# Windowed attention packed into 64 key columns from unit 3 on, and a buffer of its own for the last plain accumulators

## The chip, the cores and the metric

The program runs on one core of a Trainium2 chip. The metric is device time in microseconds (us); the kernel before takes 845.69 us (median of 3 runs, 845.41 to 848.99). TensorE (PE) multiplies matrices into PSUM, VectorE (DVE) and ScalarE (ACT) do the elementwise work, GpSimd (POOL) makes masks, and SyncE (SP) issues nearly all DMAs from one queue, in order.

## The reference

Three layers follow one another. The first is attention in which every query sees the 64 latest positions of its own sequence, itself included; the other two are feed-forward layers of 2304 tokens.

```python
batch, n_heads, seq, head_dim = (4, 8, 576, 64)
window = 64
scale = 1.0 / np.sqrt(D)
scores = scale * np.matmul(q, k.transpose(0, 1, 3, 2))
rel = pos[:, None] - pos[None, :]
mask = (rel >= 0) & (rel < window)
scores = np.where(mask, scores, -1000000000.0)
scores = scores - np.max(scores, axis=-1, keepdims=True)
attn = np.exp(scores)
attn = attn / (np.sum(attn, axis=-1, keepdims=True) + 1e-09)
x = np.matmul(attn, v)            # as 2304 tokens x 512
h = np.maximum(x @ w_in, 0.0);  x = h * h @ w_out          # d_ff 2048
h = x @ w2_in;                  out = h * np.cos(h) @ w2_out
```

## The kernel before

**The work.** The 2304 tokens are cut into nine units of 256 (n = 0 to 8). Attention runs per unit and per group of four heads (g = 0, 1): 18 calls of `attention`. Tokens of units 0 to 4 then go through the first feed-forward layer in the plain way (`UnitA`: matmuls `ph` into PSUM, a squared ReLU on ACT and DVE, matmuls `accA` into four PSUM accumulators; a block is 12 matmuls of 256 or 512 columns). Units 5 to 8 go through it in a form with fewer products (`group1` and `job1`: tiles x, y, z and `accC`), and the second layer follows in that form too (`group`, `Job`: x, y, z and `accB`). Large matmuls run as three products of high and low parts.

**One attention call.** `scores` makes S: a block of 64 queries against the 128 keys that hold its windows, 16 matmuls on quarters of the array (64 rows by 64 columns), each of which the trace records as two (32 records). `neg_max` adds a mask of 128 columns and takes the maximum (eight DVE instructions of 128x128), `exp` runs eight times over 128 columns on ACT, `recip` and `norm` follow in halves. `transp` turns each half (four transposes of 128x128 each, tile T, two groups a call), `p_copy` takes T to SBUF, and `weighted` multiplies by the values: 16 matmuls, 128 rows of keys by 64 columns, over 64 queries (tile O, 32 records). Two copies, `hi` and `lo`, put O into X; units 7 and 8 go whole into `x_whole` instead.

**The order.** The author writes operations (`op`) with engine costs and a key. A planner (`Plan.run`) sorts them into one fixed order per engine when the program is built; on the chip each engine takes its list in order and waits on semaphores. The keys of the middle stretch (attention of units 3 to 8, the sums `sums1`, the conversions `convert_w2`) stand in the table `MID`. Four PSUM banks (ring "q") are shared by S, T, O, `ph` and x, y, z; four more (ring "acc") hold accumulators, and the first `accC` takes over the banks of the last `accA`.

**The end of the plain layer.** `UnitA.finish` copies each of the four `accA` to SBUF and stores it to DRAM (`x_dram`). The copies go into ring "x2", which has two buffers: the third copy needs the first store to have landed, and the fourth the second. Ring "W" has 18 larger buffers for weights.

Of the kernel before, what the change touches and what calls it, by code (L numbers as in the profile page):

```python
# [9 lines left out]
F32 = mybir.dt.float32  # L10
# [76 lines left out]
class Plan:  # L87
# [12 lines left out]
    def op(self, engs, key, fn, deps=(), take=(), use=(), lat=None, gap=0, order=()):  # L100
        if lat is None:
            lat = self.PE_LAT if "PE" in engs else self.LAT
        o = Op(engs, key, fn, [d for d in (*deps, *order) if d is not None], list(take), lat)
        o.order = [d for d in order if d is not None]
        o.seq, o.gap = len(self.ops), gap
        self.ops.append(o)
        for b in (*take, *use):
            b.users.append(o)
        for b in take:
            b.taker = o  # L110
        o.deps += [b.taker for b in use if b.taker is not None and b.taker not in o.deps]
        return o
# [70 lines left out]
def act_us(n, sbuf=True):  # L183
    return 0.05 + 0.093 * sbuf + n / 1200.0


def dve_us(n, fast=False):
    return 0.065 + n / (1920.0 if fast else 960.0)
# [6 lines left out]
def pe_us(n, passes=1):  # L195
# [3 lines left out]


PER1 = 22.7
MID = {'att': {3: (-1.6, 1.8),
         4: (40.0, 3.7),
         5: (26.6, 6.7),
         6: (27.0, 7.3),
         7: (48.6, 4.5),
         8: (44.7, 0)},
 'sum': (13, 16, 18, 20, 24, 34, 35, 37),
 'w2': (24, 27, 29, 40, 41, 43, 45, 46, 46, 46, 46, 46, 47, 47, 48, 49),
 'w2key': 26.3}  # L210

START = {'ahead': 4,
 'att': {(0, 0): (9.7, 7.0),
# [31 lines left out]
def kernel(  # L245
# [89 lines left out]
    def bank(buf, shape, name):  # L335
        return ps_q.tile([P, *shape], F32, tag=f"q{buf.slot}", name=name)
# [264 lines left out]
    def setup_row_mask(kind):  # L601
        m = ap_.tile([P, P], F32, tag="row_mask_" + kind, bufs=1, name="row_mask_" + kind)
        nc.gpsimd.memset(m, 0.0)
        for rows in HALF:
            nc.gpsimd.affine_select(
                out=m[rows], in_=m[rows], compare_op=ALU.is_ge, fill=-BIG, base=-1,
                pattern=[[1, P]], channel_multiplier=-1,
            )
            nc.gpsimd.affine_select(
                out=m[rows], in_=m[rows], compare_op=ALU.is_ge, fill=-BIG, base=WINDOW,  # L610
                pattern=[[-1, P]], channel_multiplier=1,
            )
        if kind != "n":
            nc.gpsimd.memset(m[HALF["sb".index(kind)], 0:WINDOW], -BIG)
        masks[kind] = m

    def setup_rest(e):
        make_identity(nc, ident)
        nc.gpsimd.memset(hpi, HALF_PI)
        nc.gpsimd.memset(quarter, 0.25)  # L620
# [3 lines left out]
        o_mask[kind] = op({"POOL": 1.3}, -100, lambda e, kind=kind: setup_row_mask(kind))  # L624
    o_setup = op({"POOL": 0.8}, -100, setup_rest)
    o_mask["b"] = op({"POOL": 1.3}, -100, lambda e: setup_row_mask("b"))

    def mask_kind(t):
        if (t * P) % seq == 0:
# [16 lines left out]

    loaded = [None, None]

    def attention(n, g, key, sp, k_s=None):

        nm = f"{n}_{g}"
        t = {}
        turn = {(0, 0): "acc", (0, 1): "guest"}.get((n, g), "q")
# [151 lines left out]
        turns[turn] = o_v  # L805

        cs = slice(2 * g, 2 * g + 2)
        if n >= len(x_col):
            at = (n - len(x_col)) * UA
            new = xr.slot is None and not xr.users  # L810

            def whole(eng):
                if xr.tile is None:
                    xr.tile = wp.tile([P, NCC, H1], F32, tag=f"W{xr.slot}", name="x_whole")
                copy(eng, xr.tile[:, cs, at:at + UA], t["O"])

            o_h = op({"ACT": act_us(2 * UA, False), "DVE": dve_us(2 * UA) + 0.11}, key + sp, whole,
                     [o_v, s1_held[0]], [xr] if new else [], [ob] if new else [ob, xr])
            for r in range(2):
                x_hi[n, 2 * g + r] = x_lo[n, 2 * g + r] = o_h  # L820
            return

        half, off = divmod(x_col[n], 2 * UA)
        sl = slice(off, off + UA)

# [20 lines left out]
    class UnitA:  # L846
# [71 lines left out]
            return (b, []) if j == 0 and m % self.per == 0 else ([], b)  # L918

        def finish(self, key, ends):  # L920
            for i, b_acc in enumerate(self.acc_b):
                b = R["x2"].buf()
                t = {}
                c0 = i * self.per

                def cp_(e, i=i, t=t):
                    t["x"] = ma.tile([P, self.per, self.w], F32, tag="x2", name=f"x2_{self.n}_{i}")
                    if e == "ACT":
                        nc.scalar.activation(t["x"], self.acc[i], AF.Copy)
                    else:  # L930
                        nc.vector.tensor_copy(t["x"], self.acc[i])

                def st(e, c0=c0, t=t):
                    nc.sync.dma_start(
                        x2d[:, c0:c0 + self.per, self.n * UA:self.n * UA + self.w], t["x"])

                o = op({"ACT": act_us(512, False), "DVE": dve_us(512)}, key, cp_,
                       [ends[c0 + self.per - 1]], [b], [b_acc])
                o = dma(key, st, P * 512 * 4, [o], use=[b])
                for n in self.parts:  # L940
                    for c in range(c0, c0 + self.per):
                        x2_done[n, c] = o
# [928 lines left out]
```

## Time and profile before

| | |
|---|---|
| median of 3 runs | 845.69 us |
| the profiled execution, its own time | 845.52 us |
| its span, first to last instruction | 843.4 us |
| PE busy | 833.8 us (99%) |
| DVE busy | 656.1 us (78%) |
| ACT busy | 485.6 us (58%) |
| granted TensorE clock, mean | 0.998 |
| DMA, bytes over the span | 181.91 MB |

The span is 2.1 us shorter than the time of that execution. Busy shares are means over stages. Of the span, 0 to 100 us is the beginning (units 0 to 2, conversion of the first layer's weights), 100 to 292 us the middle (plain layer beside the attention of units 3 to 8), 292 to 475 us the first layer's second form, and from 460 us on the second layer.

### The profile page before, as it was taken

How to read it: one execution, taken by the hardware profiler on the slowest of the kernel's cores; microseconds unless marked ns; L12 is line 12 of the kernel's file. 1: busy time of each engine (PE TensorE's matmuls, PEld its weight loads, DVE VectorE, ACT ScalarE, POOL GpSimd, SP SyncE). 2: the span in 40 equal slices, each digit the busy share in tenths (PEclk: the TensorE clock that was granted, in tenths of full speed). 3: DMA queues.
4: the chain of work that ended last, by engine and by line, in shares of the span. 5: the costliest groups of instructions: out<-in, count | busy, mean ns of one | idle time of the engine just before them, and what ended most of it. 6: DMA issues, size and time to landing. Idle time of an engine off the chain costs nothing.

```text
span 843.4 us, 14086 instructions
## 1 busy us (share of the span) xinstructions
PE 833.8 (99%) x5236; PEld 730.8 (87%) x5236; DVE 656.1 (78%) x1485; ACT 485.6 (58%) x1041; POOL 11.8 (1%) x31
## 2 busy tenths in 40 slices
PE   8999999999999999999999999999999999999998
PEld 8898889998888877888888999988999988999986
DVE  6999987689777975777679788886788885788851
ACT  7998665576767744434422655653565563556542
POOL 2100010000000000000000000000000000000000
PEclk9999999999999999999999999999999999999999
DMA  9884367577775588998899495044643053643010
GB/s 343 325 328 137 141 226 270 223 235 242 289 308 187 185 296 294 349 325 304 307 356 393 172 422 192 1 169 168 227 161 126 1 205 132 249 152 112 1 38 37
DMA packets 39795, 181.91 MB, mean 216 GB/s; under 512 B 4016, under 2 KB 6576, under 8 KB 27440
## 3 DMA queue, kind: packets, MB, share of 16 engines
q1 hardware_dynamic: 39728, 181.03, 58.2%
q8 instruction: 41, 0.67, 0.3%
q14 instruction: 26, 0.21, 0.1%
HBM read 129.63 MB, written 51.38 MB: 215 GB/s over the span
## 4 chain that ended last, share of the span: by engine, by line
PE 95%; ACT 2%; DMA 2%; DVE 0%; issue 0%; SPq 0%; ACTq 0%
PE accB L1246 23%; PE ph L1577 13%; PE x L1288 12%; PE accA L909 12%; PE accC L1494 10%; PE z L1288 6%; PE x L1416 5%; PE y L1288 3%; PE z L1416 2%; PE O L776 2%; PE S L719 2%; PE T L761 2%; PE y L1416 1%; PE accA L970 1%; DMA x_dram<-x 1%; DMA qk<-in_qk_dram 1%
## 5 line engine op out<-in xcount | busy, mean ns | idle before, releaser
L1577 PE MATMUL ph<-X,W_in_w_dram 128*128 128x512 f32 (+1 forms) x624 | 125.0, 345 | 0.0
L909 PE MATMUL accA<-g,W_in_w_dram 128*128 128x512 f32 (+1 forms) x528 | 111.4, 355 | 0.0
L1577 PEld LDWEIGHTS ph<-X,W_in_w_dram 128*128 128x128 f32 x624 | 98.1, 189 | 13.8 <-issue 1.4
L1246 PE MATMUL accB<-wo,gb_e 128*128 128x512 f32 x432 | 100.1, 389 | 0.0
L909 PEld LDWEIGHTS accA<-g,W_in_w_dram 128*128 128x128 f32 x528 | 86.5, 189 | 13.7 <-issue 1.2
L1246 PEld LDWEIGHTS accB<-wo,gb_e 128*128 128x128 f32 x432 | 81.0, 188 | 16.6
L742 ACT ACTIVATE pb<-pb,mm 128x128 f32<-128x128 f32 x144 | 55.8, 389 | 13.3 <-DVE mm L736 13.3
L1246 PE MATMUL accB<-wo,gb_a 128*128 128x512 f32 x216 | 54.2, 393 | 0.0
L1246 PE MATMUL accB<-wo,gb_b 128*128 128x512 f32 x216 | 54.2, 393 | 0.0
L1246 PEld LDWEIGHTS accB<-wo,gb_b 128*128 128x128 f32 x216 | 40.2, 188 | 7.4
L373 ACT ACTIVATE raw_in_w_dram<-raw_in_w_dram 128x1024 f32<-128x1024 f32 x32 | 36.5, 1144 | 17.6 <-DMA raw_in_w_dram<-in_w_dram 17.6
L1246 PEld LDWEIGHTS accB<-wo,gb_a 128*128 128x128 f32 x216 | 40.2, 188 | 7.2
L1304 ACT ACTIVATE held<-x 128x384 f32<-128x384 f32 x72 | 34.3, 481 | 19.9 <-PE x L1288 19.8
L1288 PE MATMUL x<-X,wb 128*128 128x384 f32 x216 | 45.7, 337 | 0.0
L1288 PE MATMUL x<-X,wa 128*128 128x384 f32 x216 | 45.3, 335 | 0.0
L1494 PE MATMUL accC<-g_k,W_in_w_dram 128*128 128x512 f32 x192 | 44.3, 389 | 0.0
L1494 PEld LDWEIGHTS accC<-g_k,W_in_w_dram 128*128 128x128 f32 x192 | 36.0, 188 | 7.3
L1220 DVE TENSOR_TENSOR gb_e<-keep,gb_e 128x384 fp32r<-128x384 f32 x48 | 25.9, 554 | 20.2 <-ACT gb_e L327 20.0
L1288 PEld LDWEIGHTS x<-X,wa 128*128 128x128 f32 x216 | 38.7, 188 | 2.4
L1288 PEld LDWEIGHTS x<-X,wb 128*128 128x128 f32 x216 | 38.5, 188 | 0.3
L1435 ACT ACTIVATE held<-x 128x512 f32<-128x512 f32 x24 | 14.3, 598 | 42.2 <-PE x L1416 42.2
L873 ACT ACTIVATE r<-ph 128x512 f32<-128x512 f32 (+1 forms) x52 | 25.6, 493 | 21.1 <-PE ph L1577 20.5
(194 smaller groups left out, 1713.9 us busy)
## 6 DMA issues: line engine op xcount, KB each, us to landing
raw_in_w_dram<-in_w_dram SPq DMA_DIRECT2D x32, 1024.0 KB, 7.9
wa<-w2a_dram SPq DMA_DIRECT2D x24, 1024.0 KB, 7.7
wb<-w2b_dram SPq DMA_DIRECT2D x24, 768.0 KB, 6.6
qk<-in_qk_dram SPq DMA_DIRECT2D x17, 576.0 KB, 6.4
v<-in_v_dram SPq DMA_DIRECT2D x18, 512.0 KB, 5.9
w1s_dram<-s SPq DMA_DIRECT2D x8, 1024.0 KB, 4.7
w2a_dram<-w2a SPq DMA_DIRECT2D x8, 1024.0 KB, 6.0
w1a<-w1s_dram SPq DMA_DIRECT2D x8, 1024.0 KB, 7.7
```

The costliest lines, as they stand in the source:

```text
L373: nc.scalar.activation(hw, hw, AF.Prelu, scale=2.0**-112, alpha=-(2.0**32))
L719: nc.tensor.matmul(S[e][HALF[c], r, i], t["qk"][HALF[e], r, q0:q0 + WINDOW], t["qk"][HALF[e], r, UA + q0:UA + q0 + P], start=(r == 0 and i ...
L742: nc.scalar.activation(t["pb"][:, e, r, i], t["pb"][:, e, r, i], AF.Exp, bias=t["mm"][:, e, r, i:i + 1], scale=-1.0, accum_out=t["sm"][:, ...
L873: nc.scalar.activation(t["r"], ph()[:, 0:w], AF.Relu)
L909: nc.tensor.matmul(self.acc[i][:, k, :], w[:, j % 2, wl, m * P:m * P + P], t["g"][:, gl, :], start=(j == 0 and p == 0 and k == 0 and self. ...
L1220: nc.vector.tensor_tensor(t["g"][:, 1], r(), f32(t["g"][:, 0]), ALU.subtract)
L1246: nc.tensor.matmul(acc[0], t["g"][:, gl, m * P:m * P + P], wb.tile[:, k % 2, wl], start=(k == 0 and i == 0), stop=(k == NJ - 1 and i == 2))
L1288: nc.tensor.matmul(ps[x], wb.tile[:, i, wl, c * P:c * P + P], piece(o, c, xl), start=(first and c == 0 and k == 0), stop=(last and c == 1 ...
L1304: return b, op({"ACT": act_us(H)}, key - 6, lambda e: nc.scalar.activation(r_at(b), ps[x], AF.Copy), [dep, o_rooms], [b], [buf], lat=0.39)
L1416: nc.tensor.matmul(ps[x], wb.tile[:, i, wl, c * P:c * P + P] if src is pb or i > 1 else wb.tile[:, wl, i, c * P:c * P + P], piece1(o, c, x ...
L1494: nc.tensor.matmul(acc[0][:, 0], wb.tile[:, k % 2, wl, m * P:m * P + P], t["g"][:, gl, :], start=(k == 0 and p == 0), stop=(k == NJ - 1 an ...
L1577: nc.tensor.matmul(t["ph"][:, 0:u.w], wb.tile[:, j % 2, wl, c * P:c * P + P], u.x(xl, c), start=(c == 0 and k == 0), stop=(c == NCC - 1 an ...
```

## The change

Units 0 to 2 keep the old attention. From unit 3 on, twelve calls go to a new function `packed`. A query at place j of its block sees exactly one of the two keys j of the block before and of its own block, for every j; so the 128 columns hold 64 that count. `gather` copies, under a mask, the own-block columns over the others (and a large negative number where a sequence begins, which is in units 4 and 6), and takes the maximum over 64 columns. `exp` reads S in PSUM directly, 64 columns at a time. One group of four transposes turns everything, two products with 0/1 masks (`spread`) set the probabilities apart again, and `weighted` multiplies by the own block and the block before in turn: 32 matmuls of 64 rows by 64 columns, into two banks. Two banks mean two `hi` and two `lo` copies of half the width. In `finish`, the last unit's four copies go into one buffer of ring "W". `MID` has new keys throughout.

```diff
--- before.py
+++ after.py
@@ -199,15 +199,18 @@
 
 
 PER1 = 22.7
-MID = {'att': {3: (-1.6, 1.8),
-         4: (40.0, 3.7),
-         5: (26.6, 6.7),
-         6: (27.0, 7.3),
-         7: (48.6, 4.5),
-         8: (44.7, 0)},
- 'sum': (13, 16, 18, 20, 24, 34, 35, 37),
- 'w2': (24, 27, 29, 40, 41, 43, 45, 46, 46, 46, 46, 46, 47, 47, 48, 49),
- 'w2key': 26.3}
+PACKED = 3
+MASK = I32
+MARGIN = 0.7
+MID = {'att': {3: (-3.1, 3.1),
+         4: (38.0, 3.0),
+         5: (32.8, 5.1),
+         6: (13.5, 7.7),
+         7: (22.0, 2.0),
+         8: (19.0, 3.6)},
+ 'sum': (17, 19, 20, 25, 28, 39, 41, 42),
+ 'w2': (19, 20, 21, 40, 41, 42, 45, 48, 49, 50, 53, 55, 56, 57, 57, 58),
+ 'w2key': 65.5}
...
+    def staircase(name, dtype, cols, turned):
+        m = ap_.tile([P, cols], dtype, tag=name, bufs=1, name=name)
+        nc.gpsimd.memset(m, 1.0)
+        for rows in HALF:
+            for c in range(0, cols, WINDOW):
+                nc.gpsimd.affine_select(
+                    out=m[rows, c:c + WINDOW], in_=m[rows, c:c + WINDOW], compare_op=ALU.is_ge,
+                    fill=0.0, base=0, pattern=[[1 if turned else -1, WINDOW]],
+                    channel_multiplier=-1 if turned else 1)
+        return m
+
+    def opposite(name, dtype, m):
+        o = ap_.tile(list(m.shape), dtype, tag=name, bufs=1, name=name)
+        nc.gpsimd.tensor_scalar(o, m, -1.0, 1.0, ALU.mult, ALU.add)
+        return o
...
+    def packed(n, g, key, sp, k_s=None):
+
+        nm = f"{n}_{g}"
+        t = {}
...
+        sb = [R["q"].buf() for _ in range(2)]
+        tb = R["q"].buf()
+        ob = [R["q"].buf() for _ in range(2)]
...
+        def gather(eng, e):
+            if e == 0:
+                t["mm"] = ap_.tile([P, 2, 2, HB], F32, tag="mm", bufs=2, name=f"mm_{nm}")
+                t["sm"] = ap_.tile([P, 2, 2, HB], F32, tag="sm", bufs=2, name=f"sm_{nm}")
+            S = t["S"][e]
+            nc.vector.copy_predicated(
+                S[:, :, :, 0:WINDOW],
+                masks["own"].unsqueeze(1).unsqueeze(1).to_broadcast([P, 2, HB, WINDOW]),
+                S[:, :, :, WINDOW:P])
+            for i in range(HB):
+                kind = mask_kind(HB * n + i)
+                if kind != "n":
+                    rows = HALF["sb".index(kind)]
+                    nc.vector.copy_predicated(
+                        S[rows, :, i, 0:WINDOW],
+                        masks["prev"][rows].unsqueeze(1).to_broadcast([WINDOW, 2, WINDOW]),
+                        masks["none"][rows].unsqueeze(1).to_broadcast([WINDOW, 2, WINDOW]))
+            nc.vector.tensor_reduce(
+                t["mm"][:, e], S[:, :, :, 0:WINDOW], mybir.AxisListType.X, ALU.max, negate=True)
...
+        def exp(eng, e, r, i):
+            nc.scalar.activation(
+                t["pb"][:, e, r, i], t["S"][e][:, r, i, 0:WINDOW], AF.Exp,
+                bias=t["mm"][:, e, r, i:i + 1], scale=SCALE,
+                accum_out=t["sm"][:, e, r, i:i + 1])
...
+        def norm(eng):
+            pb = t["pb"].rearrange("p e r i q -> p (e r i) q")
+            nc.vector.tensor_tensor(
+                pb, pb, t["sm"].rearrange("p e r i -> p (e r i)").unsqueeze(2)
+                .to_broadcast([P, 4 * HB, WINDOW]), ALU.mult)
+
+        def transp(eng):
+            t["T"] = bank(tb, [2, 2, P], f"T_{nm}")
+            for e in range(2):
+                for r in range(2):
+                    nc.tensor.transpose(
+                        t["T"][:, e, r], t["pb"][:, e, r].rearrange("p i q -> p (i q)"), ident)
+
+        def spread(eng, k):
+            if k == 0:
+                t["pt"] = room("PT", ptb, 2 * DM, [2, 4, P])
+            nc.vector.tensor_tensor(
+                t["pt"][:, k], t["T"].rearrange("p e r q -> p (e r) q"),
+                masks["LU"[k]].unsqueeze(1).to_broadcast([P, 4, P]), ALU.mult)
+
+        def weighted(eng):
+            t["O"] = [bank(b, [2, P], f"O_{nm}_{i}") for i, b in enumerate(ob)]
+            for r in range(2):
+                for c in range(2):
+                    cols = slice(c * WINDOW, c * WINDOW + WINDOW)
+                    for k in range(2):
+                        for i in range(HB):
+                            for e in range(2):
+                                nc.tensor.matmul(
+                                    t["O"][i][HALF[e], r, cols],
+                                    t["v"][HALF[i], c + 1 - k + i, 2 * r + e],
+                                    t["pt"][HALF[i], k, 2 * e + r, cols],
+                                    start=(r == c == k == 0), stop=(r == c == k == 1),
+                                    skip_group_check=True)
+
...
+        late = key + sp
+        o_r = op({"DVE": 0.42}, late, recip, ex, use=[smb])
+        o_n = op({"DVE": dve_us(512) + 0.02}, late, norm, [o_r], use=[smb, pbuf], lat=MARGIN)
+        o_t = op({"PE": 4 * pe_us(P) + 0.09}, late, transp, [o_n, o_setup], [tb], [pbuf])
+        o_p = []
+        for k in range(2):
+            first = k == 0
+            o_p.append(op({"DVE": dve_us(512)}, late, lambda q, k=k: spread(q, k), [o_t, o_pack[2], *o_p],
+                          [ptb] if first else [], [tb] if first else [tb, ptb], lat=MARGIN))
+        free = ([s1_held[0]] if n >= len(x_col) else [g1_last[m] for m in x_before[n]]) if g else []
+        o_v = op({"PE": 0.35 + 16 * 0.053}, late, weighted, [l1, *o_p, *free], [*ob], [ptb, vb])
+        turns["q"] = o_v
...
     def attention(n, g, key, sp, k_s=None):
-
+        if n >= PACKED:
+            return packed(n, g, key, sp, k_s)
...
         def finish(self, key, ends):
+            apart = self.n == spans[-1][0]
+            whole = R["W"].buf() if apart else None
             for i, b_acc in enumerate(self.acc_b):
-                b = R["x2"].buf()
+                b = whole or R["x2"].buf()
                 t = {}
                 c0 = i * self.per
 
                 def cp_(e, i=i, t=t):
-                    t["x"] = ma.tile([P, self.per, self.w], F32, tag="x2", name=f"x2_{self.n}_{i}")
+                    if apart:
+                        t["x"] = part1(whole, "x2_apart", i).rearrange("p (k n) -> p k n", k=1)
+                    else:
+                        t["x"] = ma.tile([P, self.per, self.w], F32, tag="x2", name=f"x2_{self.n}_{i}")
                     if e == "ACT":
                         nc.scalar.activation(t["x"], self.acc[i], AF.Copy)
                     else:
@@ -935,7 +1142,8 @@
                         x2d[:, c0:c0 + self.per, self.n * UA:self.n * UA + self.w], t["x"])
 
...
                 o = op({"ACT": act_us(512, False), "DVE": dve_us(512)}, key, cp_,
-                       [ends[c0 + self.per - 1]], [b], [b_acc])
+                       [ends[c0 + self.per - 1]], [] if apart and i else [b],
+                       [b_acc, b] if apart and i else [b_acc])
                 o = dma(key, st, P * 512 * 4, [o], use=[b])
```

On PE, at the second call of unit 7 (names: T_7_1 is a transpose group of unit 7, group 1; O_7_1 its weighted sum; S_8_0 the next call's scores), the program before has two transpose groups, and the scores directly behind the weighted sum:

```order
L761 MATMUL T_7_1_0_3148<-ident_77,pb_7_1_3066 128x128 x4
L1577 MATMUL ph_45_3136<-X_80,W_in_w1_dram_8_962 128x512 x6
L909 MATMUL accA_3_0_2562<-g_43_3042,W_in_w1_dram_7_897 128x512 x3
...
L761 MATMUL T_7_1_1_3191<-ident_77,pb_7_1_3066 128x128 x4
L1577 MATMUL ph_46_3197<-X_80,W_in_w1_dram_10_967 128x512 x6
L776 MATMUL O_7_1_3205<-PT_7_1_3158,v_7_1_3099 64x64 x16
L719 MATMUL S_8_0_0_3223<-qk_8_0_3112 64x128 x2
```

The same place of the changed program, where the two rows of O stand eight times in all:

```order
L777 MATMUL T_7_1_3315<-ident_77,pb_7_1_3225 128x128 x4
L1111 MATMUL accA_3_3_2645<-g_44_3166,W_in_w1_dram_9_1024 128x512 x3
L1785 MATMUL ph_47_3330<-X_80,W_in_w1_dram_10_967 128x512 x9
L795 MATMUL O_7_1_0_3345<-PT_7_1_3326,v_7_1_3216 64x64 x2
L795 MATMUL O_7_1_1_3346<-PT_7_1_3326,v_7_1_3216 64x64 x2
...
L1785 MATMUL ph_47_3330<-X_80,W_in_w1_dram_10_967 128x512 x3
L1111 MATMUL accA_3_0_2623<-g_45_3268,W_in_w1_dram_9_1024 128x512 x3
L723 MATMUL S_8_0_0_3392<-qk_8_0_3253 64x128 x2
```

One transpose group is gone, O has twice the matmuls, and S no longer follows O here; each of the twelve calls' S stood directly behind the O of the call before; now five do, and seven are parted from it like this. The order and number of the large matmuls is otherwise the same, and from the first x of the second form on PE has the same list as before.

On DVE, the same call of the changed program from its scores to its transposed probabilities (g_45 and g_46 belong to the plain layer, w2a and cw to the conversion of the second layer's weights):

```order
L736 COPY_PREDICATED S_7_1_0_3226<-is_own_1436,S_7_1_0_3226 128x4x64
L748 TENSOR_REDUCE mm_7_1_3249<-S_7_1_0_3226 128x4
...
L755 TENSOR_SCALAR mm_7_1_3249<-mm_7_1_3249 128x8
L334 CAST g_45_3268<-r_45_3221 128x512
L1088 TENSOR_TENSOR g_45_3268<-r_45_3221,g_45_3268 128x512
L392 ISA cw_in_w2_dram_4_3223<-raw_in_w2_dram_4_3138,cw_in_w2_dram_4_3223 128x2048
...
L764 TENSOR_SCALAR sm_7_1_3250<-sm_7_1_3250 128x8
L765 RECIPROCAL sm_7_1_3250<-sm_7_1_3250 128x8
L769 TENSOR_TENSOR pb_7_1_3225<-pb_7_1_3225,sm_7_1_3250 128x512
...
L783 TENSOR_TENSOR PT_7_1_3326<-T_7_1_3315,by_own_1450 128x512
L783 TENSOR_TENSOR PT_7_1_3326<-T_7_1_3315,by_prev_1456 128x512
```

In place of eight masked maxima, two reciprocals and two norms stand two selections, two maxima, one reciprocal, one norm and the two products behind T.

At the end of the plain layer ACT made all four copies before (x2_3_0 to x2_3_3 are the copies of accA_3_0 to accA_3_3):

```order
L929 ACTIVATE x2_3_0_3748<-accA_3_0_2562 128x512
L327 ACTIVATE raw_in_w2_dram_7_3692<-raw_in_w2_dram_7_3692 128x1024
L929 ACTIVATE x2_3_1_3766<-accA_3_1_2569 128x512
L327 ACTIVATE g_bg0_3776<-r_bg0_3741 128x512
L929 ACTIVATE x2_3_2_3790<-accA_3_2_2584 128x512
L1435 ACTIVATE held1_3643<-x1_1_3707 128x512
L929 ACTIVATE x2_3_3_3813<-accA_3_3_2595 128x512
```

In the changed program ACT makes three of them, and the second (accA_3_1) stands on DVE, behind a weight conversion (cw) and an addition (hk1):

```order
L1602 TENSOR_TENSOR g1_ag0_3847<-r1_ag0_3840,g1_ag0_3847 128x512
L388 TENSOR_SCALAR cw_in_w2_dram_7_3861<-raw_in_w2_dram_7_3645 128x1024
L392 ISA cw_in_w2_dram_7_3861<-raw_in_w2_dram_7_3645,cw_in_w2_dram_7_3861 128x2048
L1650 TENSOR_TENSOR hk1_3777<-z1_0_3790,held1_3759 128x512
L1138 COPY x2_apart_3863<-accA_3_1_2629 128x512
```

Here g1_ag0 is the operand of the first `accC` matmuls; what moved is the copy that frees the bank of the second `accC`, from ACT to DVE.

## Rows read from the trace of the kernel before

**Rows 1.** The page, part 1: busy us (share of span) xinstructions.

```profile
PE 833.8 (99%) x5236; PEld 730.8 (87%) x5236; DVE 656.1 (78%) x1485; ACT 485.6 (58%) x1041; POOL 11.8 (1%) x31
```

**Rows 2.** Waits of PE: us in total, times, longest.

```profile
PE accC L1494 <- ACT x L929: 2.6, 1, 2.6
```

**Rows 3.** Windows, middle: busy us (xinstructions) of PE, PEld, DVE, ACT, POOL, clock, DMA.

```profile
200.00:250.00 50.00, 50.00 (x452) 40.74 (x451) 41.18 (x130) 33.63 (x98) 0.00 (x0) 1.00 0.73 276
```

**Rows 4.** Timeline of PE over one attention call: start us, us, instruction.

```profile
196.98 1.53 PE L909 MATMUL accA<-g,W_in_w_dram 128*128 128x512 f32 x6
198.35 0.60 PE L761 MATMUL T<-ident,pb 128*128 128x128 f32 x4
198.70 1.64 PE L909 MATMUL accA<-g,W_in_w_dram 128*128 128x512 f32 x6
200.18 1.55 PE L1577 MATMUL ph<-X,W_in_w_dram 128*128 128x512 f32 x6
...
201.92 1.64 PE L1577 MATMUL ph<-X,W_in_w_dram 128*128 128x512 f32 x6
203.50 1.15 PE L776 MATMUL O<-PT,v 128*64 128x64 f32 x32
204.58 1.10 PE L719 MATMUL S<-qk 64*64 64x128 f32 x32
205.61 3.03 PE L909 MATMUL accA<-g,W_in_w_dram 128*128 128x512 f32 x12
208.48 2.89 PE L1577 MATMUL ph<-X,W_in_w_dram 128*128 128x512 f32 x12
```

**Rows 5.** Windows of 20 ns inside that S: PE's (x) counts matmuls in flight.

```profile
204.82:204.84 0.02, 0.02 (x8) 0.02 (x4) 0.02 (x1) 0.02 (x2) 0.00 (x0) 1.00 0.00 0
...
204.86:204.88 0.02, 0.02 (x12) 0.02 (x8) 0.02 (x1) 0.02 (x2) 0.00 (x0) 1.00 0.00 0
...
204.92:204.94 0.02, 0.02 (x8) 0.02 (x4) 0.02 (x1) 0.02 (x1) 0.00 (x0) 1.00 0.00 0
204.96:204.98 0.02, 0.02 (x12) 0.02 (x8) 0.02 (x1) 0.02 (x1) 0.00 (x0) 1.00 0.00 0
```

**Rows 6.** Timeline of PE behind the last O, which no S follows.

```profile
278.73 3.02 PE L909 MATMUL accA<-g,W_in_w_dram 128*128 128x512 f32 x12
281.59 2.88 PE L1577 MATMUL ph<-X,W_in_w_dram 128*128 128x512 f32 x12
```

**Rows 7.** Timeline of PE at the first accC; in brackets idle time and its releaser.

```profile
314.23 0.84 PE L1494 MATMUL accC<-g_ag,W_in_w_dram 128*128 128x512 f32 x3
317.65 0.96 PE L1494 MATMUL accC<-g_ag,W_in_w_dram 128*128 128x512 f32 x3 [2.58 <-ACT x L929]
318.45 2.17 PE L1416 MATMUL x<-X,w1b 128*128 128x512 f32 x6
320.41 2.54 PE L1416 MATMUL x<-X,w1a 128*128 128x512 f32 x6
...
324.17 1.52 PE L1416 MATMUL x<-X,w1b 128*128 128x512 f32 x6
```

**Rows 8.** Windows behind that wait; the clock is the seventh column, after POOL.

```profile
320.00:322.00 2.00, 2.00 (x6) 1.61 (x5) 0.69 (x1) 0.60 (x1) 0.00 (x0) 0.50 1.01 418
```

**Rows 9.** The chain that ended last, ahead of the wait: start us, us, what.

```profile
309.61 7.30 DMA x_dram<-x
```

**Rows 10.** Groups of DVE and ACT by form: busy us, mean ns, idle before.

```profile
L736 DVE CUSTOM_DVE_ANT_0 pb<-S,row_mask_n 128x128 f32<-128x128 f32 x112 | 26.9, 285 | 4.3 <-PE S L719 4.3
L331 DVE COPY PT<-T 128x512 f32<-128x512 f32 x9 | 6.2, 690 | 4.3 <-PE T L761 4.3
L742 ACT ACTIVATE pb<-pb,mm 128x128 f32<-128x128 f32 x144 | 55.8, 389 | 13.3 <-DVE mm L736 13.3
```

**Rows 11.** Timeline of DVE, two like instructions in a row, and a conversion.

```profile
284.41 1.29 DVE L1087 TENSOR_TENSOR piece<-x_tmp,piece 128x512 fp32r<-128x512 f32 x2
309.64 1.22 DVE L389 CUSTOM_DVE_ANT_0 cw_in_w_dram<-raw_in_w_dram,cw_in_w_dram 128x2048 uint16<-128x2048 uint16 x1
```

More of the change, by code (lines that the diff above doesn't have):

```diff
@@ L615, in setup_row_mask, with setup_early, setup_first, setup_late @@
         masks[kind] = m
+    def staircase(name, dtype, cols, turned):
[12 more added lines that the diff above has]
+        return o
+    def setup_early(e):
+        masks["own"] = staircase("is_own", MASK, WINDOW, False)
+    def setup_first(e):
+        masks["prev"] = opposite("is_prev", MASK, masks["own"])
+        masks["none"] = ap_.tile([P, WINDOW], F32, tag="none", bufs=1, name="none")
+        nc.gpsimd.memset(masks["none"], -BIG / SCALE)
+    def setup_late(e):
+        masks["L"] = staircase("by_own", F32, P, True)
+        masks["U"] = opposite("by_prev", F32, masks["L"])
     def setup_rest(e):
@@ L626 @@
     o_mask["b"] = op({"POOL": 1.3}, -100, lambda e: setup_row_mask("b"))
+    o_pack = {}
     def mask_kind(t):
@@ L807, in attention @@
         cs = slice(2 * g, 2 * g + 2)
[L808 to L821, printed above, removed]
         half, off = divmod(x_col[n], 2 * UA)
@@ L926, in cp_ @@
                 def cp_(e, i=i, t=t):
-                    t["x"] = ma.tile([P, self.per, self.w], F32, tag="x2", name=f"x2_{self.n}_{i}")
+                    if apart:
+                        t["x"] = part1(whole, "x2_apart", i).rearrange("p (k n) -> p k n", k=1)
+                    else:
+                        t["x"] = ma.tile([P, self.per, self.w], F32, tag="x2", name=f"x2_{self.n}_{i}")
                     if e == "ACT":
```

80 lines of the change are left out of this document (added).

## The prediction

> **What bounds the kernel now.** I read the page first: PE is busy for 833.8 of 843.4 us [rows 1]. A busy PE need not be a fast one, so I went to PE's own waits and to its timeline. In the waits only one stop of any size stands behind the beginning: 2.6 us ahead of an `accC` [rows 2]. In the timeline the starts tell the rate: six matmuls of 512 columns take 1.37 us from start to start (196.98 to 198.35), 0.228 us each, and they go on like this from block to block [rows 4]. The middle therefore lasts as long as its PE list. The windows of the middle show DVE at 41.18 and ACT at 33.63 of 50 us [rows 3]: crowded, but ahead of PE. So the change is worth three things: what it takes from PE's list, what it does to the one stop, and what new stops it makes. What it saves on ACT or DVE gives nothing by itself.
>
> **The transposes.** From 198.35 to 200.18 PE does one transpose group and six large matmuls [rows 4]; less 1.37 us for the six, the group costs 0.46 us with what it delays behind it. Twelve calls have one group less each: 12 x 0.46 = **5.5 us gained**. No wait hides this, since PE is the engine that all wait for.
>
> **The weighted sum.** O has 32 records now, 64 columns each, and takes 1.08 us (203.50 to 204.58); S has 32 records of 128 columns on four quarters of the array and takes 1.03 us (204.58 to 205.61) [rows 4]. Per tile that is 16 records of 64 columns in 1.08 us for O on its two halves, 68 ns each, and 8 records of 128 columns in 1.03 us for S on its four quarters, 129 ns each. Both are what the columns suggest if every tile works by itself. Slices of 20 ns inside S say so directly: the number of matmuls in flight goes from 8 at 204.82 to 12 at 204.86, is back at 8 at 204.92 and again 12 at 204.96 [rows 5]. Four begin within some 50 ns, then none until the next round. The new O has 64 records of 64 columns, 16 for each of four tiles, so it should again take 16 x 68 ns = 1.08 us: **no cost**. The other bound is that a record costs PE a place of its own, whichever tile it is on; the mean of S is 1.03 / 32 = 32 ns, and 64 x 32 ns = 2.06 us, 0.98 us more per call and 11.8 us for twelve. I take the first end, as the slices show starts far denser than 32 ns.
>
> A page speaks for the other end. The Trainium skill ("TensorE: Matmul & The Clock Gate", section "Wait — 56ns, not 53.3ns?") says that matmuls never start closer than about 25 ns, however few columns they have. By that page O would take an estimated 64 x 25 ns = 1.6 us, and my sum would end at 844.2 us instead of 838.0. The slices of S do not agree with it for matmuls on different tiles; no run here yet shows 64 of them in a row.
>
> **Parted pairs.** Going into O costs 0.10 us (201.92 to 203.50 is 1.58, while the like stretch behind a transpose group, 198.70 to 200.18, is 1.48); the first twelve large matmuls behind S take 2.87 instead of 2.74, so leaving costs 0.13 [rows 4]; leaving O costs 2.86 - 2.74 = 0.12 [rows 6]. Where S no longer follows O, one more way out (0.12) and one more way in (0.10, taken from O) are paid: 7 x 0.22 = **1.5 us lost**. Bounds: 0 and 3.
>
> **The stop at accC.** From 314.23 to 324.17 PE does 24 matmuls, the three rows of six (one is left out) and two of three [rows 7]. At 0.228 us they need 5.47 us and took 9.94: 4.5 us lost. 2.58 of it is idle time. The rest is behind it: six matmuls of 512 columns take 1.96 and 2.38 us in place of 1.37, and the granted clock is 0.50, the level of 1.2 GHz, in a stretch that follows the idle time [rows 7, 8]. The releaser is the copy of an `accA` on ACT, and the chain shows what that waited for: the store of an earlier copy, 7.30 us until it landed [rows 9]. It is the ring of two buffers. With one large buffer the copies need no store, so this wait goes: **4.5 us gained**, or nothing if something else holds the copies.
>
> What is late next there is the copy of accA_3_1, which stands on DVE. From the last O to the second `accC` PE has 96 large matmuls, 96 x 0.228 + 0.12 = 22.0 us, if nothing stops it. DVE has 33 instructions of up to 512 columns and one conversion of 1.22 us to do until that copy is done, beginning about 1 us behind the last O, when that has been copied. Like instructions follow at 1.29 - 0.69 = 0.60 us, and at about 0.69 when one needs the other's result [rows 11]. That makes 1.0 + 19.8 + 1.2 = 22.0 to 1.0 + 22.8 + 1.2 = 25.0 us, so 0 to 3 us late. Four casts among the 33 are shorter; I take **0.5 us lost**.
>
> **DVE in the calls.** In seven of the twelve calls PE has only 30 to 31 large matmuls between S and T, 6.8 to 7.1 us. In that time there are two selections and two maxima over 256 elements, the scaling, eight exponentials, the reciprocal and the norm. The trace shows neither a selection nor a plain maximum; nearest is the masked maximum, 0.285 us for 128 columns [rows 10]. From there to the copy of 512 columns at 0.690 it is 1.05 ns a column [rows 10], so four over 256 are 4 x 0.42 = 1.7 us, and at twice the time per column 2.8. The exponential takes 0.389 at 128 columns [rows 10], so eight of 64 are 1.6 to 3.1 us, while DVE does other work queued ahead of the reciprocal: in the call of unit 7 a cast, a subtraction, a conversion of 1.22 us and two short sums, some 3.2 us. With 0.4 for the scaling and the reciprocal and 0.7 for the norm it comes to about 6 us, 0.5 to 1 us inside the limit. Between T and O stand 12 matmuls, 2.7 us, against T itself, 0.60 [rows 4], and two products of 0.69 (the PSUM copy of like size [rows 10]), 2.0 us. If DVE is late, O is late, and behind it stands all of PE. I take **0.5 us lost** in all; bounds 0 and about 8 (1.1 us in seven calls).
>
> The new masks are made by POOL, which is idle here (0.00 in [rows 3]); eight exponentials of half the width and split copies stay on ACT, off PE's path. The beginning and the stage behind 330 us keep their PE list.
>
> **The sum**, against the profiled execution's own 845.52 us (its span of 843.4 plus 2.1, and 0.2 below the median shown): 845.5 - 5.5 + 0 + 1.5 - 4.5 + 0.5 + 0.5 = **838.0 us**, 0.9% less.
>
> **The rivals.**
> 1. *A place for every record.* O on four tiles costs 26 ns or more per record. For it: S as a whole has 32 ns per record. Against it: [rows 5]. At 32 ns: 838.0 + 11.8 = 849.8 us, slower than before. It decides from 1.69 us per O on (7.5 / 12 = 0.63 more than 1.08).
> 2. *The buffer does nothing.* The copies wait all the same, for a place in ring "W" or behind DVE's conversion, PE idles over 2 us and its clock falls again: 838.0 + 4.0 = 842.0 us.
> 3. *DVE becomes the bound in the calls.* A selection on PSUM costs twice what I took, and seven calls hold O back by 0.6 us: 838.0 - 0.5 + 4.2 = 841.7 us. For it: DVE's 82% in [rows 3]. Against it: the number of DVE's instructions falls.
>
> **How the numbers follow.** The forecast has 0.65, rival 1 has 0.13, rival 2 0.10 and rival 3 0.12. About 0.5%, or 4.2 us, is what a measurement can tell from no change, so faster is below 841.3 and slower above 849.8. The forecast is faster in nearly all its cases, 0.62, and rivals 2 and 3 in some, 0.06; rival 1 is slower in some half of its cases, 0.07, and rival 3 in a few, 0.02; the rest is the same: 0.68, 0.23, 0.09. The likeliest case alone lies from 835 (the losses at 0) to 841. The range reaches from 834.5 up to 846, which takes in rivals 2 and 3 and the lower half of rival 1.
>
> **What would show it.** The new O at 1.1 us with 64 records (rival 1: 1.7 or more); 12 transpose groups of four instead of 24 from unit 3 on; a granted clock of 1.00 throughout 300 to 330 us, with no wait of PE on a copy; no wait of PE on DVE of over 0.5 us between 100 and 290 us; the first x of the second form some 4 us earlier than 292 us. I am wrong if O is near 2 us, if PE waits for the selections, or if a new stop stands where the old one was.

## The result, and the profile after

The changed kernel takes 838.33 us (median of 4 runs, 837.72 to 839.24) and the kernel before, beside it, 845.62 us (median of 4): a ratio of 0.9905, 95% interval 0.9879 to 0.9932. The forecast was 838.0, "faster". The profiled execution took 837.72 us, its span 836.0, at a mean granted clock of 1.0.

The page's first part shows PE still busy all the time, with 5.0 us less to do than in [rows 1], though it has 336 records more:

```profile
PE 828.8 (99%) x5572; PEld 724.5 (87%) x5572; DVE 651.0 (78%) x1338; ACT 477.0 (57%) x1048; POOL 15.6 (2%) x42
```

PE's waits behind the beginning (us in total, times, longest); the 2.6 us of [rows 2] are not among them:

```profile
PE T L777 <- DVE pb L769: 0.2, 1, 0.2
PE accC L1702 <- DVE x_apart L1138: 0.2, 1, 0.2
```

The timeline of PE over a call whose O is followed by S, to be laid beside [rows 4], and over one in which they are parted:

```profile
202.84 1.16 PE L795 MATMUL O<-PT,v 64*64 64x64 f32 x64
203.83 1.05 PE L723 MATMUL S<-qk 64*64 64x128 f32 x32
204.81 1.67 PE L1111 MATMUL accA<-g,W_in_w_dram 128*128 128x512 f32 x6
...
212.07 0.63 PE L777 MATMUL T<-ident,pb 128*128 128x128 f32 x4
212.46 3.02 PE L1785 MATMUL ph<-X,W_in_w_dram 128*128 128x512 f32 x12
...
242.44 1.16 PE L795 MATMUL O<-PT,v 64*64 64x64 f32 x64
243.54 0.97 PE L1785 MATMUL ph<-X,W_in_w_dram 128*128 128x512 f32 x3
244.34 0.86 PE L1111 MATMUL accA<-g,W_in_w_dram 128*128 128x512 f32 x3
245.13 1.10 PE L723 MATMUL S<-qk 64*64 64x128 f32 x32
246.16 2.35 PE L1111 MATMUL accA<-g,W_in_w_dram 128*128 128x512 f32 x9
```

The O of 64 records goes from 202.84 to 203.83, 0.99 us, where the O of 32 took 1.08. With S it takes 1.97 us (to 204.81), before 2.11. Parted from S, O and S and the six large matmuls between them take 3.72 us (242.44 to 246.16); less 1.37 for the six that is 2.35.

The timeline at the first `accC`, in place of [rows 7]:

```profile
288.94 1.52 PE L1624 MATMUL x<-X,w1a 128*128 128x512 f32 x6
...
306.62 0.84 PE L1702 MATMUL accC<-g_ag,W_in_w_dram 128*128 128x512 f32 x3
307.64 0.98 PE L1702 MATMUL accC<-g_ag,W_in_w_dram 128*128 128x512 f32 x3 [0.18 <-DVE x_apart L1138]
308.45 1.55 PE L1624 MATMUL x<-piece,w1a 128*128 128x512 f32 x6
309.84 1.53 PE L1624 MATMUL z<-x_more,w1a 128*128 128x512 f32 x6
```

A window of the stretch behind it has the clock (seventh column) at 1.00 where [rows 8] had 0.50:

```profile
308.00:310.00 2.00, 2.00 (x10) 1.64 (x9) 1.97 (x4) 0.51 (x2) 0.00 (x0) 1.00 0.98 391
```

And the new operations on DVE, a maximum and a selection, among its groups by form (busy us, mean ns, idle before):

```profile
L748 DVE TENSOR_REDUCE mm<-S 128x4 f32<-128x256 f32 x24 | 10.2, 424 | 0.8
L736 DVE COPY_PREDICATED S<-is_own,S 128x256 f32<-128x256 int32 x24 | 10.2, 423 | 7.3 <-PE S L723 7.2
```

**Where the time came from.** The first x of the second form starts at 288.94. In the kernel before its row is this one:

```profile
292.47 1.52 PE L1416 MATMUL x<-X,w1a 128*128 128x512 f32 x6
```

So 3.5 us come from ahead of it, the attention calls: the S of the first of the twelve calls starts at 115.30 before and at 115.37 now. The other 3.9 of the span's 7.4 come from behind it, the stop at the `accC`.

### The profile page after: what moved, and what is told of

The parts are those of the page before. It is cut to its first block, busy times and chain, and to the rows that moved or that the text cites. A ratio compares the mean times of both kernels' runs of the same rounds, so it can differ in the third digit from the quotient of the medians.

```text
span 836.0 us, 14646 instructions
## 1 busy us (share of the span) xinstructions
PE 828.8 (99%) x5572; PEld 724.5 (87%) x5572; DVE 651.0 (78%) x1338; ACT 477.0 (57%) x1048; POOL 15.6 (2%) x42
## 4 chain that ended last, share of the span: by engine, by line
PE 90%; DVE 5%; ACT 2%; DMA 1%; issue 1%; SPq 0%; ACTq 0%; DVEq 0%
PE accB L1454 24%; PE x L1496 12%; PE ph L1785 11%; PE accC L1702 10%; PE accA L1111 10%; PE z L1496 6%; PE x L1624 4%; PE y L1496 3%; PE z L1624 2%; PE O L795 1%; PE S L723 1%; PE accA L1178 1%; PE y L1624 1%; DMA qk<-in_qk_dram 1%; DMA w2b_dram<-w2b 1%; PE T L777 1%
## 5 line engine op out<-in xcount | busy, mean ns | idle before, releaser
L330 ACT ACTIVATE gb_e<-keep 128x384 fp32r<-128x384 f32 x48 | 24.2, 517 | 25.4 <-PE accB L1454 25.4
L1088 DVE TENSOR_TENSOR g<-r,g 128x512 fp32r<-128x512 f32 (+1 forms) x52 | 30.2, 581 | 6.2 <-ACT r L1083 5.4
```

What stands on the lines that cost most here:

```text
L330: nc.scalar.activation(o, i, AF.Copy, scale=scale)
L1088: nc.vector.tensor_tensor(t["g"][:, 1], t["r"], f32(t["g"][:, 0]), ALU.subtract)
```

## The experiments

The kernels of one series ran on one chip with the kernel before beside them (844.93 us in the first series, 844.83 in the second, 844.31 in the third). The last series has the changed kernel itself again; there it took 838.87 us, ratio 0.9933 (0.9921 to 0.9946), nearer to 1 than the first time and just outside what I expected of it.

> The changed kernel itself, so that the others of this series have it beside them on the same chip: ratio 0.988 to 0.993 to the kernel before.

**1. The ring back, twice.**

```diff
-            apart = self.n == spans[-1][0]
+            apart = False
```

> The changed kernel with the four last copies in the ring of two buffers again; nothing else differs. Theory (the ring alone made the stop): the third copy waits again for the first store, PE stops at an accC for 2 us or more, the granted clock falls to 0.50 behind it, and the time is 838.3 + 4.0 = 842.3 us (841.5 to 843). Rival (the new keys moved the copies apart, so that the ring no longer binds): no stop, 838.3 us.

It took 838.98 us, ratio 0.9929 (0.9914 to 0.9944), and so my theory fell: there is no stop for the ring to make. The same kernel in the last series, beside the changed one:

> The changed kernel with the ring of two buffers once more, beside the changed kernel. Theory now (with the packed calls the second store lands in 2.8 us, 0.7 us before PE needs the last bank, so the ring costs nothing in most executions): within 0.6 us of the changed kernel. Rival (the store is late in other executions than the profiled one, and the first ring run's ratio of 0.9929 beside 0.9905 was that): 1.5 us or more above it.

838.84 us, ratio 0.9934 (0.9918 to 0.9950), against 838.87: in the changed kernel the free buffer gives nothing that can be measured. The reason stands in the transfers. SP's queue before the second store and at it (start us, us, issue), in the kernel before and then with the ring back:

```profile
299.46 0.33 SPq L362 DMA_DIRECT2D raw_in_w_dram<-in_w_dram  x1
300.67 0.32 SPq L520 DMA_DIRECT2D w2a_dram<-w2a  x1
...
304.67 0.63 SPq L526 DMA_DIRECT2D w2b_dram<-w2b  x1
...
308.12 0.45 SPq L1144 DMA_DIRECT2D w1a<-w1s_dram  x1
309.61 0.32 SPq L934 DMA_DIRECT2D x_dram<-x  x1
```

```profile
305.57 0.42 SPq L1352 DMA_DIRECT2D w1a<-w1s_dram  x1
308.78 0.32 SPq L1141 DMA_DIRECT2D x_dram<-x  x1
```

Before, one step of the second layer's conversion (a load of 1 MB, stores of w2a and w2b) went out ahead of the copies' stores, and the load of w1a 1.5 us ahead of the second one. With the packed calls the conversion's stores are no longer in this stretch and w1a stands 3.2 us ahead. From 300 to 304 us the DMA engines are busy for 0.86 of the time before and for 0.00 with the ring back. The load of w1a by itself (KB, us from issue to landing) in the kernel before, where the store behind it took the 7.30 us of [rows 9], and then the load and that store with the ring back:

```profile
w1a<-w1s_dram SPq DMA_DIRECT2D x1, 1024.0 KB, 7.9
```

```profile
w1a<-w1s_dram SPq DMA_DIRECT2D x1, 1024.0 KB, 5.3
x_dram<-x SPq DMA_DIRECT2D x1, 256.0 KB, 2.7
```

The store lands 0.9 us behind that load before (316.9 and 316.0) and 0.6 us with the ring back (311.5 and 310.9). Of the 4.6 us by which it became shorter, 2.6 are the load's own (7.9 against 5.3) and 1.7 the load's longer lead. In every trace of this case the 251 transfers of this queue land in the order of their issue, so a store behind a load is done no sooner than the load.

The fourth copy, which needs the second store, begins 2.9 us behind its issue instead of 7.4 (317.00 before), in time for PE (timeline of ACT with the ring back):

```profile
311.68 0.59 ACT L1136 ACTIVATE x<-accA 128x512 f32<-128x512 f32 x1
```

PE wants the last bank 5.3 us behind the issue of that store before, and 4.2 us with the ring back. So it is not that the copies moved away from PE's need, the rival of the expectation; the store landed sooner.

**2. The buffer alone, the keys alone.** The new theory was that the stop needs both, the ring and a crowded queue. First the kernel before with the changed `finish` and nothing else:

> The kernel before with the free weight buffer for the last four copies, nothing else. Theory now (the fourth copy waits for the second store only because that store takes 7.3 us among the conversion's transfers; either a free buffer or a quiet queue ends the wait): no stop at the accC, clock 1.00 behind it, 845.6 - 4.5 = 841.1 us, ratio 0.995. Rival (the copies are held by something else too): a stop stays, 845.6 us, ratio 1.000.

841.34 us, ratio 0.9954 (0.9937 to 0.9970). The six records of `accC` between which the kernel before stopped (314.23 and 317.65 in [rows 7]) run through:

```profile
314.38 1.52 PE L1500 MATMUL accC<-g_ag,W_in_w_dram 128*128 128x512 f32 x6
```

By the traces the program takes the same time up to the first x (292.62, against 292.47) and 4.4 us less from there to its end: this is the price of the stop, clock included.

Then the kernel before with the new table `MID` and nothing else:

> The kernel before with the new table of keys, nothing else: old attention, ring of two buffers. Theory now (the keys put the second layer's conversion later, the transfers around the last copies are fewer, the store lands in about 3 us): the stop at the accC is gone though the ring is back, 841.1 us, ratio 0.995. Rival (the prediction's: the ring makes the stop whatever the keys): 845.6 us, ratio 1.000. Second rival (the new keys fit the packed calls alone, and make new stops in the old ones): over 847 us.

847.90 us, ratio 1.0034 (1.0016 to 1.0052). Here I was wrong: the keys do not quiet the queue in the old program. The stop is there, and the clock falls behind it (timeline of PE; the window's seventh column):

```profile
318.20 0.96 PE L1494 MATMUL accC<-g_ag,W_in_w_dram 128*128 128x512 f32 x3 [2.01 <-ACT x L929]
```

```profile
320.00:322.00 2.00, 2.00 (x7) 1.51 (x6) 0.35 (x1) 0.60 (x1) 0.00 (x0) 0.50 1.01 262
```

Why it is 3 us above the kernel before, which has this stop too, is not shown: no other wait of PE behind the beginning is over 0.4 us.

**3. All old keys, and the conversion's old keys.** The changed kernel with the old table:

```diff
-MID = {'att': {3: (-3.1, 3.1),
-         4: (38.0, 3.0),
...
+MID = {'att': {3: (-1.6, 1.8),
+         4: (40.0, 3.7),
```

> The changed kernel with the table of keys of the kernel before; packing and free buffer stay. Seven of the twelve calls' O are followed by S instead of five, but the last O comes only behind the first y of the second form, since T and O stand further from S than before. Theory (the gain is the transposes and the buffer; the keys only place the calls): -0.4 us for the two parted pairs less and a stop of 1 to 3 us where the second form waits for the last O's X, 839 to 841.5 us. Rival (the keys are what gained): 842 us or more, near the 845.6 of the kernel before. Second rival (the keys do nothing): 838.3 us.

848.94 us, ratio 1.0051 (1.0036 to 1.0066): packing under the old keys is slower than the kernel before. It is 10 us above the kernel with the ring in the same series. My estimate of one stop was far too low. PE's waits of 0.7 us or more behind the beginning add up to 6.4 us, all for DVE or ACT:

```profile
PE S L723 <- DVE X L854: 2.7, 1, 2.7
...
PE x L1624 <- DVE piece L1295: 1.2, 1, 1.2
PE accC L1702 <- DVE g_k L1602: 1.0, 1, 1.0
...
PE T L777 <- ACT w2a L330: 0.8, 1, 0.8
PE x L1624 <- ACT piece L330: 0.7, 1, 0.7
```

Some 3 us more go with the clock, which is at 0.50 behind the longest of them (a window; the clock is the seventh column):

```profile
184.00:190.00 6.00, 5.46 (x38) 4.55 (x39) 3.30 (x10) 0.59 (x1) 0.00 (x0) 0.50 1.00 327
```

Then only the lines `'w2'` and `'w2key'` old, with the buffer and with the ring:

> The changed kernel with the conversion of the second layer's weights at its old keys; the keys of the attention and the sums stay new, and the free buffer stays. Theory (the packed calls need the new attention keys, and the buffer takes the transfers out of the way of the copies): no stop at the accC, under 1 us more than the changed kernel, ratio to before 0.990 to 0.993. Rival (the conversion beside the calls makes DVE late, as with all old keys): stops ahead of T, O or S of over 0.5 us, ratio 0.995 or more.

> The same with the ring of two buffers back, so that the conversion's transfers and the ring meet again. Theory (ring and traffic together make the stop): the second store takes 5 to 8 us again, PE stops 1.5 to 3 us at an accC, the clock falls to 0.50 behind it, 3 to 5 us more than with the buffer. Rival (the stop hung on the attention's keys or on which engine makes the copies): no stop, the same time as with the buffer.

839.27 us, ratio 0.9933 (0.9911 to 0.9956), and 840.97 us, ratio 0.9947 (0.9931 to 0.9964). So it is the attention's keys (with the sums') that the packed calls need, not the conversion's. With the ring the stop is 0.4 us instead of the 1.5 to 3 that I expected; with the buffer there is none. The two intervals overlap, and the profiled execution of the ring has a wait for `pb` of 1.5 us, some 50 us ahead of the copies, so the times of this pair are inconclusive. Its transfers tell more. With the ring the conversion's stores went out 18 us ahead of the copies', and the load of w1a 1.2 us ahead of the second store; that store took 5.1 us, landing 0.6 us behind the load, and the fourth copy waited for it:

```profile
w1a<-w1s_dram SPq DMA_DIRECT2D x1, 1024.0 KB, 5.6
x_dram<-x SPq DMA_DIRECT2D x1, 256.0 KB, 5.1
```

A load that goes out shortly before the store is thus enough for a stop, if a small one; it does not take the conversion's stores.

**4. The weighted sum on one tile at a time.**

```diff
-            for r in range(2):
-                for c in range(2):
-                    cols = slice(c * WINDOW, c * WINDOW + WINDOW)
-                    for k in range(2):
-                        for i in range(HB):
-                            for e in range(2):
+            for i in range(HB):
+                for e in range(2):
+                    for r in range(2):
+                        for c in range(2):
+                            cols = slice(c * WINDOW, c * WINDOW + WINDOW)
+                            for k in range(2):
```

> The changed kernel with the 64 records of each O in another order: the 16 records of one tile of the array come in a row, then those of the next, where before the four tiles took turns. Same products, same sums. Theory (each tile works by itself, and O is short only because four tiles work at once): 64 records in a row at 68 ns each make O 4.35 us instead of 1.08, 3.3 us more in twelve calls, 838.3 + 39 = 877 us. Rival (a record costs PE 17 ns wherever it goes): O stays at 1.1 us and the time at 838.3 us.

863.68 us, ratio 1.0224 (1.0204 to 1.0245), 24.7 us above the kernel with the ring in the same series, 2.1 us for each O. A parted O of this kernel lasts 3.40 us in place of 1.10 (the other parted ones 3.33 or 3.34):

```profile
164.24 3.47 PE L795 MATMUL O<-PT,v 64*64 64x64 f32 x64
167.64 0.62 PE L1785 MATMUL ph<-X,W_in_w_dram 128*128 128x256 f32 x3
```

The mechanism is right (the same 64 records cost three times as much when the tiles don't take turns), the size was not: 3.40 / 64 = 53 ns a record, not 68. The 68 held the way into O as well (0.10 of the 1.08 us, 6 ns a record); what makes up the rest was not tried.

**5. The transposes twice.**

```diff
-            for e in range(2):
+            for e in [0, 1, 0, 1]:
                 for r in range(2):
                     nc.tensor.transpose(
```

> The changed kernel with the four transposes of each of the twelve calls made twice into the same tile T; the order of all else is the same. Theory (PE is what all wait for, so a transpose costs what it takes there): four more in a row cost 0.35 us, from the start of a group to the start of the next matmul, so 12 x 0.35 = 4.2 us more, 842.5 us (841.8 to 844; with 0.46, a whole group's price, 843.9). Rival (the transposes lie in gaps of PE, and what was gained came from DVE's shorter list): under 1 us more, 838.3 to 839.3 us.

842.43 us, ratio 0.9976 (0.9965 to 0.9987), 3.45 us above the kernel with the ring. A group of eight takes 0.79 us from its start to the next matmul, one of four 0.39 (212.07 to 212.46 above):

```profile
214.67 1.04 PE L777 MATMUL T<-ident,pb 128*128 128x128 f32 x8
215.46 2.99 PE L1785 MATMUL ph<-X,W_in_w_dram 128*128 128x512 f32 x12
```

That is 12 x 0.40 = 4.8 us by these rows and 3.45 by the times. By the starts in the two traces the stretch from the S of the first packed call to the first x grows by 4.0 us (173.85 to 177.85), so most of what a transpose lasts is a cost to PE.

**6. No margin for DVE.**

```diff
-MARGIN = 0.7
+MARGIN = 0.15
```

> The changed kernel planned with 0.15 us instead of 0.7 between DVE's norm, the two products behind T and what PE does with them; nothing else. T to O then has 9 large matmuls in five calls, 2.05 us, where the transposes and two products need 0.6 + 2 x 0.69 = 2.0 and what DVE has queued ahead of them. Theory (DVE is close behind PE in the calls, the prediction's third rival in small): PE waits for PT and pb for 0.3 to 1 us in half of the calls, 2 to 5 us in all, 840.5 to 843 us. Rival (DVE has room, the margin does nothing): within 0.6 us of the changed kernel.

854.44 us, ratio 1.0129 (1.0106 to 1.0152): 15.6 us above the changed kernel, three times the most that I gave it (5 us). The waits of PE (us in total, times, longest), and a stretch of PE and one of DVE ahead of the worst of them:

```profile
PE ph L1785 <- DVE X L854: 4.9, 3, 3.6
PE accC L1702 <- ACT x_apart L1136: 2.1, 1, 2.1
...
PE T L777 <- DVE pb L769: 1.0, 3, 0.4
```

```profile
174.60 1.16 PE L795 MATMUL O<-PT,v 64*64 64x64 f32 x64
...
181.16 2.26 PE L1785 MATMUL ph<-X,W_in_w_dram 128*128 128x256 f32 x12 [3.62 <-DVE X L854]
```

```profile
174.56 1.21 DVE L392 CUSTOM_DVE_ANT_0 cw_in_w_dram<-raw_in_w_dram,cw_in_w_dram 128x2048 uint16<-128x2048 uint16 x1
...
176.53 1.22 DVE L438 TENSOR_TENSOR w2o<-cw_in_w_dram,w2o 128x1024 fp32r<-128x1024 f32 x1
...
180.26 0.75 DVE L854 TENSOR_TENSOR X<-O,X 128x256 fp32r<-128x256 f32 x2
```

O ends at 175.8, but its low half X is the last in DVE's list, behind the conversion (1.21, 1.22) and the next call's selections and maxima; a `ph` that needs it waits until 181.16. The waits for `pb`, which I had expected, are the small ones. And the `accC` waits 2.1 us though its copies have the free buffer: three of them stand on ACT behind the rounding of a weight that had not been loaded yet (timeline of ACT):

```profile
317.68 1.10 ACT L376 ACTIVATE raw_in_w_dram<-raw_in_w_dram 128x1024 f32<-128x1024 f32 x1 [2.95 <-DMA raw_in_w_dram<-in_w_dram]
...
319.70 1.56 ACT L1136 ACTIVATE x_apart<-accA 128x512 f32<-128x512 f32 x3
```

This is the second rival of the prediction ("the copies wait all the same"), in a program planned with less room. All waits behind the beginning come to 10.7 us; the clock, at 0.50 from 182 to 185 and from 322 to 325 us, behind the two longest, accounts for some 3 more, and the rest stays open.

**7. A candidate: unit 2 packed too, and the last copies on ACT alone.**

```diff
-PACKED = 3
+PACKED = 2
...
-                o = op({"ACT": act_us(512, False), "DVE": dve_us(512)}, key, cp_,
+                o = op({"ACT": act_us(512, False)} if apart else {"ACT": act_us(512, False), "DVE": dve_us(512)}, key, cp_,
```

> The changed kernel with unit 2 packed as well (two calls more), and the four last copies on ACT alone. Theory (a transpose group that is left out gives 0.46 us wherever PE is what all wait for, and the accC's copy is no longer late): 2 x 0.46 + 0.5 = 1.4 us less than the changed kernel. Rival (unit 2's calls stand where the beginning is bound by loads and DVE, so the groups give nothing): 0 to 0.5 us less. Second rival (POOL's masks and the four times longer chain of norm, transposes and products stop PE in unit 2): slower than the changed kernel.

841.75 us, ratio 0.9967 (0.9955 to 0.9979), 2.9 us above the changed kernel. PE waits 2.3 us for X again, and at the `accC` 0.6 us for ACT where it waited 0.2 for DVE:

```profile
PE ph L1785 <- DVE X L854: 2.3, 2, 1.4
...
PE accC L1702 <- ACT x_apart L1136: 0.6, 1, 0.6
```

The two edits were made in one run, so these waits are all that tells their shares. None of the kernels tried beats the changed one.

## Why the prediction was right, and where it was not

**The transposes (-5.5): right, as far as shown.** Experiment 5 puts a group at 0.29 to 0.40 us without its way in and out, where the rows of before gave 0.35 without and 0.46 with it. The difference, 0.11 us a group, was not tried by itself.

**The weighted sum (no cost): right, for the reason given.** 64 records in 0.99 us are 15.5 ns a record, and experiment 4 shows that it is the tiles' taking turns that makes it so. The rival of a place for every record at 32 ns is dead (where the prediction lets it decide, from 1.69 us per O on, its own sum gives 1.71). The trace does not agree with the 25 ns or so of the Trainium skill ("TensorE: Matmul & The Clock Gate", section "Wait — 56ns, not 53.3ns?") for matmuls on four tiles: by it O would be an estimated 1.6 us, and it is 0.99.

**Parted pairs (+1.5): right in size.** A parted pair takes 2.35 us against 2.11 for O and S before, 0.24 each, 1.7 for seven. What I left out is that four of the five pairs that stayed together became shorter, 1.97: 0.6 us gained (the fifth has the last O of the old kind). With the transposes and DVE's half microsecond the sum ahead of the first x was -3.5, and the rows say -3.5; so about as much as the four pairs gained was lost in places that no single row shows, and that the sum comes out to the tenth is in part luck.

**The stop at accC (-4.5): right in size, wrong in what the change owes it to.** The step "with one large buffer the copies need no store, so this wait goes" is true of the kernel before (experiment 2), but in the changed kernel the wait would have gone without the buffer (experiment 1). I took the 7.30 us of the store in [rows 9] as given, and it hung on what was issued ahead of it: the stop needed the ring and a late store together. In the traces the store lands just behind the load of w1a, in every program; how late that is depends on how long the load takes and how far ahead it went out. No run moved the load alone. In the three programs with the old calls (before, and experiment 2) the conversion's stores of w2a and w2b go out between 300 and 307 us; in the changed one and in those of experiments 1 and 3 they don't, whichever keys stand in `MID`. With less margin (experiment 6) they go out at 299.56 and 302.61, but there the copies' stores begin 12 us later. So it goes with the packed calls; what in them moved the stores was not tried. The size is that of the profiled execution, and experiment 2 confirms it there (4.4 us by the traces). But in 44 later executions of the kernel before, 23 had a mean clock of 1.000 and a median of 844.13 us, 21 a lower one and 845.75. The first are still 2.8 us above the kernel with the buffer alone (841.34, in one of those series), which is about the idle time of the stop; the other 1.6 us go with the lower clock, and the profiled execution (0.998) was of the second kind. This may be part of why the second measurement gives 0.9933.

**The copy of accA_3_1 (+0.5): right.** From 306.62 to 309.84 twelve matmuls take 3.22 us in place of 12 x 0.228 = 2.74.

**DVE in the calls (+0.5): right in size, by less room than the bounds said.** A selection and a maximum are 0.42 us each, as estimated, and only one T waits, 0.2 us. But the upper bound of 8 us was too low and in the wrong place: with DVE later the loss is 15.6 us (experiment 6) or 10 us (experiment 3), some 3 us of each by the lower clock behind the stops. The longest waits come where X is late for `ph` or for S, a subtraction behind O that I had not followed. The keys, which the prediction took as given in the order, are what keeps this away; packing with the old ones is slower than the kernel before.

## What to carry to other kernels

Where a wait ends with a transfer, ask what went out ahead of it in the same queue before pricing a buffer: here the buffer alone was enough (experiment 2), and where the load ahead landed early the buffer was worth nothing (experiment 1). Where PE is the bound and another engine is close behind, follow every result that PE's list needs, the last one behind a product too (here the low half X), since 0.55 us in the plan decided over 10 us (experiment 6). Small matmuls on separate tiles of the array should take turns; the same ones in a row cost three times as much.

## What the runs showed of the hardware that was not expected

O on four tiles is shorter with 64 records (0.99 us) than on two halves with 32 (1.08), and 3.40 us with the same 64 in a row. A store of 256 KB took 7.30 us in one program and 2.7 us in another, each time landing 0.6 to 0.9 us behind a load of 1 MB that SP had issued ahead of it; all 251 transfers of that queue landed in the order of their issue, in every trace. And behind a stop of 2.6 us the granted clock was 0.50 in the profiled execution, while the mean clock is 1.000 in 23 of 44 executions of the same program; no trace here is of such an execution, so whether its stop is shorter stays open.
